# A gated mix of windowed attention and a ReGLU layer, forward and backward: other lengths in the build-time planner, e^z spread by DRAM instead of matmuls

## The chip, the cores and the metric

One core of a Trainium2 chip runs the whole kernel in one launch. The metric is the device time of that launch in microseconds (us). A core has five engines that run side by side, each through its own instruction stream in a fixed order: TensorE (PE, matmuls into eight PSUM banks of 128 x 512 float32), VectorE (DVE), ScalarE (ACT), GpSimd (POOL), and SyncE (SP), which here does nothing but issue transfers. ScalarE and GpSimd issue some transfers too. Transfers run on 16 DMA engines. Engines wait for one another, and for transfers, on semaphores.

## The reference

Sequence S = 2048, width D = 512, 32 heads of 16, a causal window of 256, F = 1376, everything bfloat16.

```python
def attn(x, wqkv, wo):                       # 32 heads, Dh = 16
    q, k, v = split_heads(x @ wqkv)
    scores = (q @ k.T) * Dh ** -0.5          # masked to 0 <= i - j < 256
    return merge_heads(softmax(scores) @ v) @ wo

def ffn(x, W_gate, W_up, W_down):
    gate, up = x @ W_gate, x @ W_up
    return (gate * (gate > 0) * up) @ W_down

z = (x * gate_w).sum(-1, keepdims=True)
g = sigmoid(z)
out = g * attn(x, wqkv, wo) + (1 - g) * ffn(x, W_gate, W_up, W_down)
```

The kernel returns `out` (out_0) and, for a given grad_out, the gradients by x (out_1), wqkv (out_2), wo (out_3), W_gate and W_up (out_4, out_5), W_down (out_6) and gate_w (out_7).

## The kernel before

**The order is planned when the kernel is built.** The Python code doesn't issue instructions one after the other. It lists operations (`op`, `dma`) with what they read and write, a rank (lower goes first), and a length in ns for each engine that could do them, and the method `run` of class `Flow` (L274) plays them in a small event model: an engine that is free takes the ready operation with the lowest rank, an operation counts as done after its length and a `LATENCY` of its engine, and a transfer counts as done when a common DMA clock has moved its bytes (at 240 bytes per ns) and 2300 ns have passed. The order in which the model starts the operations becomes the fixed order of each engine's stream on the chip. So a length in the code changes no instruction, only where it stands, and on which engine where two were given (`either`: ScalarE or VectorE). TensorE's operations have a mode: "row" (scores, one operation is a `slot`), "col" (sweeps) and "den" (dense); a change of mode costs `SWITCH` in the model. The rank of a dense operation gets a small random addition from the list `SEEDS`, one seed for every 200 operations. Where the model has nothing else for TensorE, it puts in a filler matmul (L1569) into a free bank.

**Buffers** are rings in one SBUF tile, `arena`, and the PSUM tile `banks`; an operation that opens a buffer waits in the model until an old one is done. In the profile nearly everything is therefore called `arena` or `banks`, and lines and tile shapes tell operations apart.

**Start (about 0 to 40 us).** The 2048 rows are four blocks `sb` of 512. For each block the kernel loads x (`x_r`) and grad_out (`db_r`), turns x with TensorE into `x_T` (`rows_to_T`), computes z by 16 narrow matmuls (`zf` in `gates`), and on ScalarE e^z, ln(1 + e^z) and 1 - g (`ez_all`, `g_all`, `omg_all`, one number per row, rows on partitions, L840). VectorE multiplies grad_out by 1 - g in place (`sf`, L848), and TensorE turns it into `db_T`. `proj` (L799 to L809) projects 128 columns (8 heads) of K, V and Q out of `x_T` and dO out of `db_T` (by wo), and stores them to DRAM in a layout by heads: `KV_d` and `QD_d`. Since db holds (1 - g) grad_out and the attention's share is g grad_out, the projected dO is multiplied by e^z = g / (1 - g) on the way out of PSUM (L799, VectorE). There rows lie along the columns, so e^z is needed on every partition: `ez_bc`, 128 x 2048. To get it, `gates` lets TensorE multiply `gw_rep` (gate_w repeated in 128 columns) with `x_T`, four matmuls of 512 columns for a block, and ScalarE takes the exponential of the bank (L860):

```python
accumulate(pz, [mm(lambda: pz[:], lambda c=c: gw_rep[:, c, :], lambda c=c: x_T[:, c, sl]) for c in range(DC)],
           [(x_T, sb), gw_rep], 0.8 if sb else 1.6)
op({ACTE: t_act(W)}, lambda e: nc.scalar.activation(ez_bc[:, sl], pz[:], ACT.Exp), r=[pz], w=[(ez_bc, sb)], rank=1)
```

**Attention (about 40 to 709 us).** 16 stages n: four groups of 8 heads, in halves of four heads with four blocks of rows each. `load_stage` loads a stage's K and V (`KV_d`, L975), Q and dO (`QD_d`, L978) and a turned copy by a DMA transpose (L980), from which GpSimd or VectorE copies V beside a column of ones (L987). Work comes in slots (L1049): one slot holds the eight score matmuls of a unit that begins (Q K) and of one that ends (dO V), two heads each, in two units that lie in other rows of the array where possible. After a slot ScalarE takes the exponentials (L1090), GpSimd masks the edge blocks (L1066), VectorE multiplies by the dO V scores (L1096). Sweeps (L1112) are the products of these probabilities with V, Q, K and dO. Between them the model sets dense work: the projections of the other head groups, the gated layer (`front`, L673, L897, L902; `back`), whose activations go through `ffn_d`, and the early products of the last stage (`accumulate_pairs`, L1402).

**End (about 709 to 806 us).** Dense products only: the heads' results come back from `HD_d` by transposes on ScalarE's queue, L1402 forms o and dx for each tile t of 128 rows, partial sums come from `b_d` and `dx_p`; `final` and `whole` finish a tile and store it (L1517 and L1564 are the last stores; GpSimd's additions are L1509 and L1515). The gradient of gate_w is a sum over all 2048 rows: for 13 of the 16 tiles VectorE adds them up in `gx` over the columns' rows (the long sum), which is split into a bfloat16 part and its remainder (`gx2`, the subtraction is L1474 on GpSimd here), and `direct` (L1481) adds both halves and the last three tiles by five matmuls of one bank, copied out (L651, 1 x 512) and stored at the very end.

**Queues.** SP issues nearly all transfers, in the planned order; its issue of a transfer that waits for data holds up all that stand behind it.

Of the kernel before, what the change touches and what calls it, by code (L numbers as in the profile page):

```python
# [10 lines left out]
ALU = mybir.AluOpType  # L11
# [23 lines left out]
def place(segs, dist):  # L35
# [15 lines left out]
LATENCY = {PE: 230, DVE: 130, ACTE: 150, POOL: 100, SP: 2300}  # L51
SWITCH = 98
BACKLOG = 1500
# [3 lines left out]
    51316, 1683, 24937, 57401, 42949, 47415, 22897, 43060, 3505, 15123, 3852, 2860, 11922, 41846, 5348, 49132,  # L57
    25696, 10850, 43592, 31894, 31367, 38632, 11354, 8520, 40074, 25554, 54658,
# [157 lines left out]
class Flow:  # L216
# [57 lines left out]
    def run(self):  # L274
# [3 lines left out]
        now, dma_free, mode, heavy, done = 0.0, 0.0, "", False, 0  # L278
# [42 lines left out]
        while done < len(self.ops):  # L321
            progress = True
            while progress:
                progress = False
                for e in (PE, ACTE, DVE, POOL, SP):
# [3 lines left out]
                    if dma_free > now + BACKLOG:  # L329
                        cands = [o for o in cands if o.rank < 3 or not o.nbytes]  # L330
# [36 lines left out]
                    if o.nbytes:  # L367
                        dma_free = max(dma_free, now + took) + o.nbytes / 240
# [31 lines left out]
def kernel(  # L400
# [42 lines left out]
    MASKV = {DVE: 470, ACTE: 600}  # L443
    DTT = 640
    HQ, OUTS, DIRECT = (SP, ACTE), 2, 3
    COLX, ROWX = 20, 4
# [4 lines left out]
    PAD = 0  # L451
    FRONT, EARLY, BACK, DW, DWO, LAG = 4, 4.6, 4.3, 4.4, 4.5, 3
# [16 lines left out]
    dx_p = [Buf(None, dram.tile([P, D], F32, name=f"dx_p{t}")) for t in range(NT)]  # L469

# [246 lines left out]
    def load_rows(dst, src_d, sb):  # L717
        dma(lambda: nc.sync.dma_start(dst[:, 4 * sb:4 * sb + 4, :],
                                      src_d[sb * W:(sb + 1) * W, :].rearrange("(t p) d -> p t d", p=P)),
            w=[(dst, sb)], nbytes=512 * KB, rank=3)  # L720
# [40 lines left out]
    for sb in range(1, NSB):  # L761
        load_rows(x_r, x_d, sb)
        load_rows(db_r, go_d, sb)
# [48 lines left out]
    def proj_weights(c, deps=()):  # L812
        w3, woT = wsets.pop(("p", c)) if c else wsets["pw", c]
        wi = buf("wi")
        op({POOL: 1200}, lambda e: nc.gpsimd.tensor_copy(wi[:].rearrange("p c (h w d) -> p c w h d", w=2, d=Dh)[:, :, 0],
                                                         w3[:, :, 1, :].rearrange("p c (h d) -> p c h d", d=Dh)),
           r=[(w3, 1)], w=[(wi, 0)], rank=3, deps=deps)
        op({POOL: 1200}, lambda e: nc.gpsimd.tensor_copy(wi[:].rearrange("p c (h w d) -> p c w h d", w=2, d=Dh)[:, :, 1],
# [6 lines left out]
    def gates(sb):  # L825
# [11 lines left out]
        op({PE: 16 * 17}, zf, r=[(x_T, sb), gw_out], w=[zps], rank=0.5 if sb else 1.6, mode="den")  # L837
# [12 lines left out]
        op({DVE: 4 * 200}, sf, r=[gate_b, (db_r, sb)], w=[(db_r, sb)], rank=0)  # L850
# [13 lines left out]
    for sb in range(NSB):  # L864
        later[sb] = rows_to_T(x_T, x_r, sb, 0.2)
# [6 lines left out]
        later["db", sb] = rows_to_T(db_T, db_r, sb, 0.4)  # L872
        proj(0, 3, sb, 1)
    load_ffn(0, [later[0]])
    proj_weights(0, [later["db",3]])

    def front(fc):
        fs = fsz(fc)
        wg, wu, wdT = wsets.pop(("f", fc))
        for tg in range(NSB):  # L880
# [16 lines left out]
            op({DVE: t_stt(W)}, lambda e, q=q, ups=ups: nc.vector.scalar_tensor_tensor(  # L897
# [3 lines left out]
            for k, (a, b) in enumerate((("rg", "upm"), ("dhs", "upm"), ("dhs", "rg"))):  # L901
                op({POOL: t_pool(W, 2), DVE: DTT}, lambda e, q=q, k=k, a=a, b=b: EN[e].tensor_tensor(  # L902
# [68 lines left out]
    def load_stage(n):  # L971
# [15 lines left out]
        op({POOL: 330, DVE: 200}, lambda e: EN[e].tensor_copy(v_of(k1r), v_of(kvr)), r=[kvr, k1r], w=[k1r], rank=1.2)  # L987
# [17 lines left out]
    def units(kind, n):  # L1005
# [9 lines left out]
        for k in range(2 * len(packs)):  # L1015
            u = Unit()
            u.segs, u.runs, width = packs[k // 2]
            u.kind, u.n, u.p, u.r, u.width = kind, n, k // 2, k % 2, width * P
            u.last = k == 2 * len(packs) - 1
            u.Pt = buf("Pt" + kind)  # L1020
            u.S = [buf("S") for _ in range(2)]
            u.dP = u.Pd = None
            us.append(u)
        return us

    def users(kind, n):
        return sets[kind, n] + (sets["A", n + 1][:2] if kind == "N" and joined(n + 1) else [])
# [5 lines left out]
    def score_mms(u, second):  # L1033
# [3 lines left out]
        for i in (2 * u.r, 2 * u.r + 1):  # L1037
            rs = slice(32 * i, 32 * i + (32 if second else Dh))
            lst = []
            for a, b0, cnt, col, kind, n in u.segs:  # L1040
# [6 lines left out]
                def one(lt=lt, ls=ls, rt=rt, rsl=rsl, i=i, rs=rs, cs=slice(col * P, (col + cnt) * P)):  # L1047
                    bank = u.dP[i % 2][:, cs] if second else u.S[i % 2][:, cs]
# [13 lines left out]

    def mask(u):
        for kind, b, cnt, sgn in u.runs:
# [6 lines left out]
    def slot(nxt, cur):  # L1071

        if cur:
            cur.Pd, cur.dP = buf("Pd"), [buf("dP") for _ in range(2)]
        lists, ins, outs = [], [], []
        for u, second in ((cur, True), (nxt, False)):
            if u:
# [9 lines left out]
        if nxt:  # L1087
            w = nxt.width
            for h in range(2):
                op({ACTE: t_act(w)}, lambda e, h=h: nc.scalar.activation(nxt.Pt[:, h, :w], nxt.S[h][:, :w], ACT.Exp),  # L1090
                   r=[nxt.S[h]], w=[(nxt.Pt, h)], rank=0)
            op({POOL: sum(t_pool(2 * cnt * P) for _, _, cnt, _ in nxt.runs)}, lambda e: mask(nxt), r=[nxt.Pt], w=[nxt.Pt], rank=0)
        if cur:
            wc = cur.width
            for h in range(2):
# [502 lines left out]
```

## Time and profile before

| | us |
|---|---|
| three runs, median (lowest to highest) | 805.25 (804.71 to 806.75) |
| the profiled execution, its own time | 807.78 |
| its span, from the first to the last instruction | 806.1 |
| TensorE's share of its full clock in it | 0.999 |
| DMA, bytes moved (mean rate) | 152.18 MB (189 GB/s) |
| scores L1049, TensorE busy (2944 matmuls) | 156.4 |
| sweeps L1112, TensorE busy (2944 matmuls) | 94.6 |
| dense L673, TensorE busy (2000 matmuls) | 393.6 |
| dense pairs L1402, TensorE busy (784 matmuls) | 186.2 |
| score products L1096 on VectorE (740) | 458.2 |
| exponentials L1090 on ScalarE (740) | 395.3 |
| masks L1066 on GpSimd (752) | 354.9 |

The busy times are sums over an engine's instructions; matmuls are pipelined and their ends are modelled, so the sums say how long TensorE had something in it, and the distances between the starts of successive matmuls say how fast it went. The profiled execution is 2.5 us longer than the median of the others; sums made on its trace are therefore compared with its own time, and moved to the median by that difference.

In the lines that follow, `PE`, `DVE`, `ACT`, `POOL` are engines, `SPq` is the issue of a transfer on SP; a line of the timeline gives the start in us, the length in us, engine, line of the code, operation, what is written and read. The lines by stretch give for each the length, the busy time (and count) of PE, weight loads, DVE, ACT and POOL, the granted clock, the share of the DMA engines and their GB/s. The lines of TensorE's waits give the total in us, the count and the longest.

### The profile page before, as it was taken

The page shows a single profiled execution, that of the slowest core. Times are in us where ns is not written, and L with a number is a line of the kernel's source. Part 1 is how long each engine was busy: PE and PEld are TensorE (multiplying, and loading weights), DVE is VectorE, ACT ScalarE, POOL GpSimd, SP SyncE. Part 2 cuts the span into 40 slices and gives each one's busy share as a digit, 9 for nine tenths or more (in the row PEclk, how much of TensorE's full clock was granted, in tenths as well). Part 3 has the DMA queues.
Part 4 walks back from the last instruction along what each step waited for, and adds up shares of the span by engine and source line. Part 5 has one row for each costly group of instructions (what it writes and reads, how often), then busy time and mean ns, then how long its engine had stood idle before and what let it go on. Part 6 is the DMA issues. An engine that isn't in the chain of part 4 may idle for free.

```text
span 806.1 us, 24249 instructions
## 1 busy us (share of the span) xinstructions
PE 791.7 (98%) x8946; PEld 370.9 (46%) x8946; DVE 697.5 (87%) x1249; ACT 600.7 (75%) x1200; POOL 547.5 (68%) x957
## 2 busy tenths in 40 slices
PE   8999999999999999999999999999999999999997
PEld 5543444454354454454545545443434443344443
DVE  3589999999999999999999988999999999927654
ACT  5787798788888788888887888888988888413232
POOL 2388878766898888989997765657666666202246
PEclk9999999999999999999999999999999999999999
DMA  9889558576789887989898798768746766688886
GB/s 241 195 161 243 144 149 183 135 158 129 172 184 217 185 155 190 228 202 198 204 237 190 214 205 173 159 164 207 211 124 155 201 194 143 192 247 211 219 230 202
DMA packets 313009, 152.18 MB, mean 189 GB/s; under 512 B 203161, under 2 KB 303194, under 8 KB 312250
## 3 DMA queue, kind: packets, MB, share of 16 engines
q1 hardware_dynamic: 293938, 136.47, 72.8%
q10 hardware_dynamic: 18456, 12.72, 5.7%
q0 software_dynamic: 496, 1.44, 0.7%
q8 instruction: 70, 1.15, 0.6%
q14 instruction: 49, 0.40, 0.2%
HBM read 55.02 MB, written 55.74 MB: 137 GB/s over the span
## 4 chain that ended last, share of the span: by engine, by line
PE 59%; DMA 5%; POOL 4%; DVE 3%; issue 2%; ACT 2%; SPq 0%; POOLq 0%; DVEq 0%; ACTq 0%
PE banks L673 24%; PE banks L1402 16%; PE banks L1049 11%; PE banks L1112 7%; DMA arena<-b_d 2%; DVE arena L1096 1%; POOL arena L1066 1%; DMA arena<-dx_p 1%; POOL arena L902 1%; ACT arena L1090 1%; POOL arena L1515 1%; DMA arena<-HD_d 1%; PE banks L1147 1%; POOL arena L1509 1%; DMA out_dram<-arena 1%
## 5 line engine op out<-in xcount | busy, mean ns | idle before, releaser
L1096 DVE TENSOR_TENSOR arena<-arena,banks 128x512 bf16<-128x512 bf16 (+1 forms) x740 | 458.2, 665 | 24.4 <-PE banks L1049 21.5
L1066 POOL TENSOR_SCALAR_AFFINE_SELECT arena<-arena 128x256 bf16<-128x256 bf16 (+1 forms) x752 | 354.9, 497 | 151.1 <-ACT arena L1090 132.5
L1090 ACT ACTIVATE arena<-banks 128x512 bf16<-128x512 f32 (+1 forms) x740 | 395.3, 588 | 76.8 <-PE banks L1049 59.4
L673 PE MATMUL banks<-arena 128*128 128x512 bf16 (+4 forms) x2000 | 393.6, 336 | 1.1 <-ACT arena L1090 0.9
L673 PEld LDWEIGHTS <-arena 128*128 128x128 bf16 (+1 forms) x2000 | 175.0, 98 | 154.3 <-issue 55.1
L1402 PE MATMUL banks<-arena 128*128 128x512 bf16 (+1 forms) x784 | 186.2, 380 | 0.0
L1049 PE MATMUL banks<-arena 32*128 32x128 bf16 (+5 forms) x2944 | 156.4, 270 | 4.2 <-DMA arena<-QD_d 1.4
L1049 PEld LDWEIGHTS <-arena 32*128 32x128 bf16 (+1 forms) x2944 | 48.8, 92 | 140.6 <-issue 136.9
L1402 PEld LDWEIGHTS <-arena 128*128 128x128 bf16 (+1 forms) x784 | 69.4, 97 | 89.4 <-issue 17.1
L902 POOL TENSOR_TENSOR arena<-arena 128x512 bf16<-128x512 bf16 (+1 forms) x90 | 104.4, 1164 | 3.8 <-ACT arena L651 1.7
L651 ACT CAST arena<-banks 128x512 bf16<-128x512 f32 (+4 forms) x162 | 77.2, 489 | 31.9 <-PE banks L673 16.2
L1112 PE MATMUL banks<-arena 128*32 128x128 bf16 (+5 forms) x2944 | 94.6, 271 | 1.8 <-POOL arena L987 1.7
L1112 PEld LDWEIGHTS <-arena 128*32 128x32 bf16 (+1 forms) x2944 | 60.5, 94 | 34.6 <-issue 15.9
L1509 POOL TENSOR_TENSOR arena<-arena 128x512 bf16<-128x512 f32 x12 | 16.1, 1341 | 52.1 <-DMA arena<-b_d 26.2
L1143 POOL TENSOR_TENSOR arena<-arena 128x512 bf16<-128x512 f32 x32 | 37.3, 1166 | 11.6 <-issue 8.3
L1508 ACT ACTIVATE arena<-banks,g_all 128x512 f32<-128x512 f32 x12 | 8.2, 688 | 32.1 <-DMA arena<-dx_p 9.8
L902 DVE TENSOR_TENSOR arena<-arena 128x512 bf16<-128x512 bf16 (+1 forms) x42 | 31.3, 749 | 0.4 <-ACT arena L651 0.2
L897 DVE SCALAR_TENSOR_TENSOR arena<-arena,banks 128x512 bf16<-128x512 bf16 (+1 forms) x44 | 29.8, 678 | 1.2 <-PE banks L673 0.8
L653 DVE CAST arena<-banks 128x512 bf16<-128x512 f32 (+1 forms) x38 | 24.4, 644 | 4.1 <-PE banks L673 3.2
L1512 ACT COPY arena<-banks 128x512 f32<-128x512 f32 x12 | 6.9, 587 | 25.0 <-POOL arena L1515 17.0
L1149 DVE SCALAR_TENSOR_TENSOR arena<-arena,vec,banks 128x512 bf16<-128x512 bf16 x32 | 23.6, 737 | 1.4 <-PE banks L1147 1.3
L1141 DVE SCALAR_TENSOR_TENSOR arena<-banks,vec,arena 128x512 bf16<-128x512 f32 x32 | 23.8, 744 | 1.0 <-ACT arena L1140 0.7
(94 smaller groups left out, 403.1 us busy)
## 6 DMA issues: line engine op xcount, KB each, us to landing
ffn_d<-arena SPq DMA_DIRECT2D x40, 384.0 KB
arena<-ffn_d SPq DMA_DIRECT2D x88, 128.0 KB
out_dram<-arena SPq DMA_DIRECT2D x66, 128.0 KB
arena<-HD_d ACTq DMA_DIRECT2D x28, 256.0 KB
KV_d<-arena SPq DMA_DIRECT2D x32, 128.0 KB
QD_d<-arena SPq DMA_DIRECT2D x32, 128.0 KB
arena<-KV_d SPq DMA_DIRECT2D x32, 128.0 KB
arena<-QD_d SPq DMA_DIRECT2D x32, 128.0 KB
```

The lines of the kernel that those rows point to most:

```text
L651: nc.scalar.copy(out, in_)
L653: EN[e].tensor_copy(out, in_)
L673: return lambda start, stop: nc.tensor.matmul(out_fn(), lhsT=lhs_fn(), rhs=rhs_fn(), start=start, stop=stop)
L897: op({DVE: t_stt(W)}, lambda e, q=q, ups=ups: nc.vector.scalar_tensor_tensor(out=q["upm"][:fs, :], in0=q["rg"][:fs, :], scalar=0.0, in1=up ...
L902: op({POOL: t_pool(W, 2), DVE: DTT}, lambda e, q=q, k=k, a=a, b=b: EN[e].tensor_tensor(out=q["act"][:fs, k, :], in0=q[a][:fs, :], in1=q[b] ...
L1049: nc.tensor.matmul(bank, lhsT=lt[rs, ls], rhs=rt[rs, rsl], start=True, stop=True)
L1066: nc.gpsimd.affine_select(out=v.rearrange("p h (b k) -> p h b k", b=cnt), in_=v.rearrange("p h (b k) -> p h b k", b=cnt), compare_op=ALU.i ...
L1090: op({ACTE: t_act(w)}, lambda e, h=h: nc.scalar.activation(nxt.Pt[:, h, :w], nxt.S[h][:, :w], ACT.Exp), r=[nxt.S[h]], w=[(nxt.Pt, h)], rank=0)
L1096: op({DVE: t_dve(wc)}, lambda e, h=h: nc.vector.tensor_tensor(out=cur.Pd[:, h, :wc], in0=cur.Pt[:, h, :wc], in1=cur.dP[h][:, :wc], op=ALU. ...
L1112: nc.tensor.matmul(acc[32 * i:32 * i + wt.shape[1], q0:q0 + cnt * P], lhsT=wt, rhs=m[:, i % 2, col * P:(col + cnt) * P], start=(k == 0), s ...
L1143: op({POOL: t_pool(W, 2), DVE: t_dve(W)}, lambda e: EN[e].tensor_tensor(out=U[:], in0=ri[:], in1=qd[:], op=ALU.mult), r=[ri, qd], w=[U], r ...
L1402: nc.tensor.matmul(bank[:], lhsT=l_(), rhs=r_(), start=(lo + k == 0), stop=(lo + k == n - 1))
```

## The change

1. **The model's numbers.** Latencies, the cost of a switch, and the lengths of a dozen operations are other numbers; transfers issued by GpSimd get a DMA clock of their own, and one that lies beside such a transfer is slower in the model.
2. **e^z for dO** (`EZD = 1`). For each block, SP stores the four columns of `ez_all` to a DRAM buffer `ez_d` of 512 float32, and loads it back to all 128 partitions of `ez_bc`. The four matmuls and the exponential of 128 x 512 of each block are not issued any more (the early `return`); `gw_rep` is still made.
3. **The gate's long sum**: its two matmuls (`direct` on `gx2`) are listed after all tiles, and so come last of the five in the accumulation.
4. **The copies of the projection weights** (`proj_weights`) and the load of the second head group wait for another operation: the turning of grad_out's block 2 instead of block 3 (and of x's).
5. **New seeds**, and so another random addition to every dense operation's rank.
6. **Knobs**: `ROWQ`, `END2`, `START2`, `WIDE`, `TD`, `TDB`, `F0`, `F1`, and slots, units and sweeps rewritten so that a unit may hold both sides of the array. With the values given (`WIDE = 0`, `END2 = 0`, `START2 = 0`, `TD = TDB = 4`, `ROWQ = 9`, `F0 = 0`, `F1 = 1`) they issue what was issued before.

```diff
-LATENCY = {PE: 230, DVE: 130, ACTE: 150, POOL: 100, SP: 2300}
-SWITCH = 98
-BACKLOG = 1500
+LATENCY = {PE: 230, DVE: 135, ACTE: 165, POOL: 100, SP: 2300}
+SWITCH = 97
+BACKLOG, RATE, BY_POOL, BESIDE = 1500, 240, 200, 100
...
 SEEDS = (
-    51316, 1683, 24937, 57401, 42949, 47415, 22897, 43060, 3505, 15123, 3852, 2860, 11922, 41846, 5348, 49132,
+    17664, 1835, 46651, 26643, 54718, 39605, 56992, 30299, 25672, 29398, 19980, 44718, 38679, 30873, 39266, 39201,
...
-                    if dma_free > now + BACKLOG:
+                    if dma_free > now + BACKLOG and e != POOL:
                         cands = [o for o in cands if o.rank < 3 or not o.nbytes]
...
-                    if o.nbytes:
-                        dma_free = max(dma_free, now + took) + o.nbytes / 240
+                    if o.nbytes and e == POOL:
+                        pool_free = max(pool_free, now + took) + o.nbytes / BY_POOL
+                        post(pool_free + LATENCY[SP], "done", o)
+                    elif o.nbytes:
+                        begin = max(dma_free, now + took)
+                        lap = min(max(0, pool_free - begin), o.nbytes / BESIDE)
+                        dma_free = begin + lap + (o.nbytes - lap * BESIDE) / RATE
                         post(dma_free + LATENCY[SP], "done", o)
...
-    MASKV = {DVE: 470, ACTE: 600}
+    MASKV = {DVE: 490, ACTE: 710}
-    COLX, ROWX = 20, 4
+    COLX, ROWX = 3.5, 2.4
...
+    ez_d = [Buf(None, dram.tile([W], F32, name=f"ez_d{sb}")) for sb in range(NSB)]
...
-        op({POOL: 1200}, lambda e: nc.gpsimd.tensor_copy(wi[:].rearrange("p c (h w d) -> p c w h d", w=2, d=Dh)[:, :, 0],
+        op({POOL: 660}, lambda e: nc.gpsimd.tensor_copy(wi[:].rearrange("p c (h w d) -> p c w h d", w=2, d=Dh)[:, :, 0],
...
-        op({PE: 16 * 17}, zf, r=[(x_T, sb), gw_out], w=[zps], rank=0.5 if sb else 1.6, mode="den")
+        op({PE: 16 * 25}, zf, r=[(x_T, sb), gw_out], w=[zps], rank=0.5 if sb else 1.6, mode="den")
...
-        op({DVE: 4 * 200}, sf, r=[gate_b, (db_r, sb)], w=[(db_r, sb)], rank=0)
+        op({DVE: 1060}, sf, r=[gate_b, (db_r, sb)], w=[(db_r, sb)], rank=0)
...
+        sl = slice(sb * W, (sb + 1) * W)
+        if EZD:
+            dma(lambda: nc.sync.dma_start(ez_d[sb][:].rearrange("(t p) -> p t", p=P), ez_all[:, cs_]), deps=[a], w=[ez_d[sb]],
+                nbytes=16 * KB, rank=1)
+            dma(lambda: nc.sync.dma_start(ez_bc[:, sl], ez_d[sb][:].partition_broadcast(P)), r=[ez_d[sb]], w=[(ez_bc, sb)],
+                nbytes=256 * KB, row=2048, rank=1.2)
+            return
         pz = buf("acc")
-        sl = slice(sb * W, (sb + 1) * W)
         accumulate(pz, [mm(lambda: pz[:], lambda c=c: gw_rep[:, c, :], lambda c=c: x_T[:, c, sl]) for c in range(DC)],
...
-    proj_weights(0, [later["db",3]])
+    proj_weights(0, [later["db", 2]])
...
-                op({POOL: t_pool(W, 2), DVE: DTT}, lambda e, q=q, k=k, a=a, b=b: EN[e].tensor_tensor(
+                op({POOL: t_pool(W, 2), DVE: 700}, lambda e, q=q, k=k, a=a, b=b: EN[e].tensor_tensor(
...
-        cols = sum(2 * u.width for u in (cur, nxt) if u) * (2 if nxt and cur and nxt.r == cur.r else 1)
-        wsets["row"] = op({PE: cols / 9.6 + ROWX * count}, lambda e: weave(lists), r=ins, w=outs, order=[prev] if prev else [],
+        wsets["row"] = op({PE: max(cols) / 2.4 + ROWX * count}, lambda e: weave(lists), r=ins, w=outs, order=[prev] if prev else [],
...
-        load_proj(c, [later[3]] if c == 1 else ())
+        load_proj(c, [later["db", 2]] if c == 1 else ())
...
-            for k in range(2):
-                direct(lambda: ones_c[:], lambda k=k: gx2[:, k], [(gx2, k)])
...
+    for k in range(2):
+        direct(lambda: ones_c[:], lambda k=k: gx2[:, k], [(gx2, k)])
     dgs = buf("dgs", [1, D])
```

More of the change, by code (lines that the diff above doesn't have):

```diff
@@ L451 @@
     PAD = 0
+    ROWQ = 9
+    END2 = 0
+    START2 = 0
+    WIDE = 0
+    EZD = 1
+    TD = 4
+    TDB = 4
+    F0 = 0
+    F1 = 1
     FRONT, EARLY, BACK, DW, DWO, LAG = 4, 4.6, 4.3, 4.4, 4.5, 3
@@ L1061, in weave, with part @@
             k += 1
+    def part(u, t_, b):
+        return t_[:, b % 2, b // 2 * u.width:(b // 2 + 1) * u.width]
     def mask(u):
-        for kind, b, cnt, sgn in u.runs:
+        for k, (kind, b, cnt, sgn) in [(k, run) for k in range(len(u.rs)) for run in u.runs]:
+            b += k * u.width // P
             v = u.Pt[:, :, b * P:(b + cnt) * P]
@@ L1093, in slot @@
-        if cur:
-            wc = cur.width
-            for h in range(2):
-                op({DVE: t_dve(wc)}, lambda e, h=h: nc.vector.tensor_tensor(
-                    out=cur.Pd[:, h, :wc], in0=cur.Pt[:, h, :wc], in1=cur.dP[h][:, :wc], op=ALU.mult),
-                    r=[cur.Pt, cur.dP[h]], w=[cur.Pd], rank=0)
+        for u in nxts:
+            for b, bank_ in enumerate(u.S):
+                op({ACTE: t_act(u.width)}, lambda e, u=u, b=b, bank_=bank_: nc.scalar.activation(
+                    part(u, u.Pt, b), bank_[:, :u.width], ACT.Exp), r=[bank_], w=[(u.Pt, b)], rank=0)
+            op({POOL: sum(t_pool(2 * cnt * P) for _, _, cnt, _ in u.runs) * len(u.rs)}, lambda e, u=u: mask(u), r=[u.Pt], w=[u.Pt], rank=0)
@@ L1257 @@
                 tasks_A2(cur.n)
-            elif cur.kind == "A" and cur.j == 1 and joined(cur.n):
+            elif cur.end:
                 tasks_N(cur.n - 1)
```

157 lines of the change are left out of this document (96 added, 61 removed).

## The prediction, made before the changed kernel was run

> **What bounds the kernel now.** I read the busy times first, then the same by stage, the chain of waits, TensorE's own waits, and last the timelines of the start and of the end.
>
> ```profile
> span 806.1 us, 24249 instructions
> PE 791.7 (98%) x8946; PEld 370.9 (46%) x8946; DVE 697.5 (87%) x1249; ACT 600.7 (75%) x1200; POOL 547.5 (68%) x957
> ```
> ```profile
> 0.00:40.00 40.00, 35.72 (x343) 22.11 (x343) 17.74 (x48) 25.10 (x51) 13.38 (x36) 1.00 0.88 218
> 40.00:709.00 669.00, 663.21 (x8168) 305.71 (x8161) 630.16 (x1100) 551.33 (x1097) 499.52 (x896) 1.00 0.80 183
> 709.00:806.00 97.00, 92.79 (x448) 43.04 (x444) 49.59 (x101) 24.23 (x52) 34.57 (x26) 0.99 0.81 220
> ```
> ```profile
> 709.05 37.47 PE banks L1402 x173
> ```
>
> TensorE is busy in all three stages (start, attention, last dense products) at full clock. The piece of the chain gives the price of a 512-column matmul in a stream: 37.47 / 173 = 0.217 us. Since a matmul's end is modelled, I also walked the starts of all 8946 matmuls in the timeline, in which each shape has a regular step (512 columns 0.216, 384 columns 0.163, 256 columns 0.109, eight score matmuls of one slot 0.329, a change from dense work to scores 0.095). The regular steps add up to 778.0 us from the first start to the last, and the starts lie 799.8 us apart: 21.8 us are gaps. Some 6 us of these lie in the first 40 us (slow steps up to 9 us, a wait for x of 1.5, the wait shown below), eight gaps over 0.35 us between 40 and 720 us make 7.9 us, a dozen slots whose two units share the same rows of the array 2.6 us, and from 720 us on there are none. So a TensorE microsecond that is taken away is worth a microsecond, unless a gap takes its place; only gaps can turn the result.
>
> ```profile
> PE banks L1112 <- POOL arena L987: 1.7, 1, 1.7
> PE banks L1049 <- DMA arena<-QD_d: 1.4, 1, 1.4
> PE banks L1049 <- DVE arena L1141: 1.3, 1, 1.3
> PE banks L673 <- ACT arena L1090: 0.9, 1, 0.9
> ```
> The reader should see that these are single events, and that each names a late transfer or an engine behind one: L987 copies V out of a transfer from KV_d.
>
> **The change, part by part.** *Removed: sixteen matmuls.* In `gates`, 4 blocks x 4 matmuls of 512 columns that spread z = x.gate_w over 128 partitions, with 4 exponentials (L860). 16 x 0.217 = 3.5 us of TensorE, all of it on the path. ScalarE's 4 x 0.60 us are hidden: in the first 40 us it is busy 25.1.
>
> *Added: eight transfers on SP.* For each block a store of 128 x 4 numbers to `ez_d` and a load of 2 KB to each of 128 partitions. On SP a store like it (QD_d, below) takes about 0.6 us to issue and a plain load 0.34 to 0.53: 4 x 1.0 = 4 us of SP over the first 40 us. The loads bring 1 MB; at the 218 GB/s of this stage that is 4.8 us of the DMA engines, which are at 0.88 there. What waits for it is this:
>
> ```profile
> 13.12 0.60 ACT L860 ACTIVATE arena<-banks 128x512 f32<-128x512 f32 x1
> 22.00 1.29 SPq L809 DMA_DIRECT2D QD_d<-arena  x2
> 23.33 0.53 SPq L718 DMA_DIRECT2D arena<-in_grad_out_dram  x1
> 28.71 0.34 SPq L978 DMA_DIRECT2D arena<-QD_d  x1
> 31.47 1.14 DVE L848 TENSOR_SCALAR arena<-arena,omg_all 128x512 bf16<-128x512 bf16 x4 [1.07 <-DMA arena<-in_grad_out_dram]
> 33.57 0.41 PE L1049 MATMUL banks<-arena 16*128 16x384 bf16 x8 [1.41 <-DMA arena<-QD_d]
> ```
>
> Now e^z of block 0 is there at 13.72. VectorE multiplies it into the projected dO (L799, 21.1), the product goes to QD_d (22.0 to 23.3), and the load of 28.71 brings it back for the first scores at 33.57. In the new order of SP, e^z's store for block 0 stands behind three stores of K, V, Q; its load behind two 512 KB loads, a K/V load, a DMA transpose and the store for block 1; the dO part's store behind the store for block 2; and the load of QD_d eight transfers later, past the dO load of block 3 and a transpose. Behind the waiting multiply on VectorE stand the scaling of dO block 2 and a copy that frees a bank of TensorE's.
>
> The first scores are matmul 283 now, after 25.9 us of regular steps, and TensorE is ready for them at 32.1. In the new order they are matmul 277, after 24.6 us: ready at 30.8. The way there: e^z's store at about 12.8 (its exponential follows the same matmuls as L840 now); its load behind the transpose that now ends issuing at 18.7 and the store for block 1, so about 19.4; 4 to 5 us to land, as the QD_d load of 28.71 needs 4.9; the multiply, 0.7, to 24.2; its store 0.6 and 3 to 6 us to land (now 22.7 to 28.7 at most); the load 3 to 5 us. That puts the first scores between 30.8 (no wait, if the loads are short) and 36. I take 33.3: a wait of 2.5 where it is 1.5 now, **+1.0**. From below: the wait goes altogether, -1.5. From above: both trips take 8.1 us each, as the dO load of 23.33 does that L848 waits for at 31.47; that is the slower rival.
>
> The Trainium skill (DMA: Bandwidth & Descriptors, Rules for kernel authors) says that a transfer whose last dimension is strided becomes one descriptor per element, and tells authors to rearrange it. That speaks against the store to `ez_d`: 512 pieces of 4 bytes. No row of this trace shows such a store. As an estimate, at the 32 ns that a packet takes on queue 1 on average (72.8% of 16 engines over 806.1 us for 293938 packets) it holds each engine for 1.0 us; by this rule the sum below would be -2.8 and the time 802.4.
>
> *Moved: the whole order.* The planner's lengths and seeds change no instruction, only where it stands. I counted both built orders. TensorE keeps 2944 score and 2944 sweep matmuls; its runs of one kind go from 821 to 818, fewer sweeps are split (87 to 78 runs), more changes go from dense work to scores (330 to 338). In regular steps the new order is 3.9 us shorter up to the last matmul that is needed, so **-0.4** beside the sixteen matmuls. Whether the gaps between 40 and 720 us grow is the unknown. I counted for every transfer how much TensorE work lies between the last matmul that it needs and the first that needs it. Past the start, room under 7 us is left 4 times now and 5 times then, under 9 us 23 and 22 times. The K/V transpose with 6.3 to 7.4 us of room stays the tightest kind. So I take **0** for these gaps, with -4 (half of them gone) and +4 (half as many again) as ends. VectorE, at 630 of 669 us in this stage, keeps its 740 score products; its count changes by ten instructions.
>
> *Moved: the gate's long sum.* The five matmuls of the gate's gradient end TensorE's work in both orders, so this puts no work on the path. But the subtraction ahead of them leaves GpSimd for VectorE:
>
> ```profile
> 785.07 1.16 POOL L1474 TENSOR_TENSOR arena<-arena 128x512 bf16<-128x512 f32 x1 [3.47 <-PE banks L1402]
> 800.78 1.26 POOL L1515 TENSOR_TENSOR arena<-arena 128x512 bf16<-128x512 f32 x1
> 800.85 0.57 ACT L651 CAST arena<-banks 1x512 bf16<-1x512 f32 x1 [0.59 <-PE banks L1481]
> 802.07 0.33 SPq L1517 DMA_DIRECT2D out_dram<-arena  x1
> 803.26 0.43 SPq L1564 DMA_DIRECT2D out_dram<-arena  x1
> ```
> GpSimd's last addition ends at 802.04; SP waits for it before it can issue the two last stores. The gradient is copied by 801.42; without that wait its store could go 1.8 us earlier. GpSimd loses 1.16 us and a wait in that chain; I take half, **-0.9** (ends 0 and -1.8). The reader should also see what is late next: the last transpose of HD_d now issues 44 us before the end (761.64) and is used at 775.3. In the new order it can't issue before a store that needs work 13 us of TensorE ahead of its use, where it now has 14. That still covers it.
>
> **The sum**: -3.5 - 0.4 - 0.9 + 1.0 = **-3.8 us**, against the span of 806.1 (1.7 us lie around it, 807.78 in that execution): 802.3. The three unprofiled runs have a median of 805.25, so **801.4**.
>
> **The rivals.** *(B) The better lengths also shorten the gaps.* The eight gaps are places where the planner expected an engine earlier: 7.9 us, half of them gone is -4, and **797.4**. For: one of them is a multiplication on VectorE planned at 640 ns and now at 700. Against: the others hang on transfers, and the rate of SP's transfers stays at 240 in the model.
>
> *(C) The start takes the saving back.* The first scores come at 36.2, 5.4 us after TensorE is ready: +3.9, nothing left, **805.2**. For: DMA at 0.88 and SP in order. Against: e^z of the first block has 8 us until the dO product needs it.
>
> *(D) Slower: e^z's two trips are late.* If both take 8.1 us, the load lands at 19.4 + 8.1 = 27.5 (the store is back by 20.9, and 1.5 of that is lost as well: 29.0), the product is stored by 30.3, lands by 36 and is loaded by 40.9: a wait of 10.1 instead of 1.5, so -3.5 - 0.4 - 0.9 + 8.6 = +3.8: **809.1**. It turns slower where the first scores start after 36.2, and by 0.3% after 38.6. For: the 8.1 us of the dO load in this very stretch. Against: that load moves 512 KB, e^z's 256 KB. The Trainium skill (TensorE: Matmul & The Clock Gate, The HAM clock gate) adds that an idle window of about 3.4 us halves the clock; by it this case would be worse by up to 1.7 us. The trace can't show it: its waits are 1.7 us at most and the clock stays at 1.00.
>
> **Chances.** Forecast 0.52 (799 to 803.5), B 0.17, C 0.17, D 0.14. What this kernel's measurement can tell is 0.3%, 2.4 us. Faster by more (below 802.8): 0.45 of the forecast, B, 0.02 of C: 0.64. Slower by more (above 807.7): 0.13 of D. The rest is 0.23. The range takes in B's middle and C with the lower part of D: 796 to 807.
>
> **What would show it.** Sixteen dense matmuls of 512 columns fewer in the group of L673; no exponentials of 512 columns in `gates`; first scores near 33 us; the wait for QD_d 1 to 4 us; gaps between 40 and 720 us of 8 us together; the last store issued less than a microsecond after the gradient's copy. The prediction is wrong if the first scores start after 36 us, if single waits of TensorE in the attention stage add up to more than 12 us or less than 4, or if TensorE stands still in the last 90 us.

## The result, and the profile after

The changed kernel takes **844.07 us** (median of 4 runs, 837.37 to 849.42), the kernel before beside it 805.50 us (4 runs, 804.71 to 806.75): a ratio of 1.047 with a 95% interval of 1.039 to 1.055. The forecast was 801.4 us. Rival D, the slower one, was given 809.1 us, 3.8 us more than before; what came is ten times that, 38.6 us more. The profiled execution took 846.16 us with a span of 844.5.

Busy times, then the same by stage (length, busy time and count of PE, weight loads, DVE, ACT and POOL, granted clock, share of the DMA engines, GB/s), then TensorE's waits, all of the changed kernel:

```profile
span 844.5 us, 24068 instructions
PE 788.8 (93%) x8822; PEld 372.6 (44%) x8929; DVE 697.1 (83%) x1256; ACT 596.0 (71%) x1187; POOL 548.3 (65%) x959
```
```profile
0.00:40.00 40.00, 24.03 (x210) 16.35 (x214) 10.29 (x33) 13.65 (x26) 9.26 (x25) 0.87 0.96 149
40.00:100.00 60.00, 39.27 (x273) 16.87 (x274) 26.25 (x47) 27.52 (x53) 24.95 (x45) 0.80 0.97 144
100.00:747.00 647.00, 632.17 (x7871) 296.00 (x7967) 611.67 (x1069) 531.64 (x1061) 479.46 (x864) 1.00 0.76 181
747.00:845.00 98.00, 93.38 (x475) 43.41 (x475) 48.94 (x109) 23.14 (x48) 34.60 (x25) 1.00 0.90 222
```
```profile
PE banks L1089 <- DMA arena<-QD_d: 14.1, 1, 14.1
PE banks L793 <- DMA arena<-in_A_x_dram: 7.6, 3, 5.8
PE banks L793 <- DVE arena L868: 6.3, 1, 6.3
PE banks L689 <- DMA arena<-in_B_W_down_dram: 5.1, 1, 5.1
```
```profile
62.55 0.62 PE L1089 MATMUL banks<-arena 16*128 16x384 bf16 x8 [14.06 <-DMA arena<-QD_d]
```

TensorE is busy 24.0 of the first 40 us (before: 35.7) and 39.3 of the next 60 (before: 60.0 of that stretch). Yet the DMA engines are at 0.96 and 0.97 while they move 149 and 144 GB/s: before they moved 218 GB/s at 0.88. So packets take up their time, yet little moves. The share adds up the times of all packets, so it can pass 1 where these overlap. The first scores (the last line) wait 14.1 us for QD_d; they start at 62.55 us instead of 33.57. And the clock, which stood at 1.00 before, is granted at 0.87 and 0.80.

The walk along the starts of TensorE's matmuls, as in the prediction, puts the difference into four parts (us; a matmul whose record is missing is counted by its regular step; the tail is from the last matmul's start to the end of the span):

| | before | after | difference | predicted |
|---|---|---|---|---|
| regular steps | 777.8 | 773.7 | -4.1 | -3.9 |
| gaps, 0 to 100 us | 7.2 | 47.7 | +40.5 | +1.0 |
| gaps, later | 14.8 | 18.9 | +4.1 | 0 (-4 to +4) |
| tail | 4.7 | 2.6 | -2.1 | -0.9 |

The loss is in the start. These are the transfers of e^z on SP in the changed kernel (start of the issue in us, its length), transfers of QD_d beside them, and the three multiplies on VectorE that wait for e^z (the last bracket is the idle time ahead):

```profile
13.04 0.42 SPq L878 DMA_DIRECT2D ez_d<-ez_all  x1
...
22.55 0.57 SPq L878 DMA_DIRECT2D ez_d<-ez_all  x1
24.44 0.34 SPq L880 DMA_DIRECT2D arena<-ez_d  x1
24.88 0.62 SPq L829 DMA_DIRECT2D QD_d<-arena  x1
...
38.31 0.34 SPq L880 DMA_DIRECT2D arena<-ez_d  x1
38.74 0.57 SPq L878 DMA_DIRECT2D ez_d<-ez_all  x1
39.36 1.62 SPq L829 DMA_DIRECT2D QD_d<-arena  x2
...
59.19 0.34 SPq L1013 DMA_DIRECT2D arena<-QD_d  x1
```
```profile
38.49 0.69 DVE L819 TENSOR_TENSOR arena<-banks,arena 128x512 bf16<-128x512 f32 x1 [8.92 <-DMA arena<-ez_d]
...
51.80 0.69 DVE L819 TENSOR_TENSOR arena<-banks,arena 128x512 bf16<-128x512 f32 x1 [7.99 <-DMA arena<-ez_d]
...
63.18 0.69 DVE L819 TENSOR_TENSOR arena<-banks,arena 128x512 bf16<-128x512 f32 x1 [0.21 <-DMA arena<-ez_d]
```

The first store of 2 KB is issued at 13.04, and its load can go at 24.44: the store landed at 24.43, 11.4 us after its issue. The next three took 15.7, 19.9 and 12.5 us. Meanwhile other transfers are slow as well. The first load of e^z lands at 38.40, 14.0 us after its issue. Block 0's dO can then be multiplied (38.49); its store, the first of the two issued from 39.36, lands at 59.12, 19.8 us later. The load for the first scores goes at 59.19 and lands at 62.50. A store to QD_d that doesn't need e^z, issued at 24.88, lands at 40.41. In the trace's records of single packets, the 1,160 packets of 1 KB that start between 10 and 14 us take 53 ns each on average; after a burst of 4-byte packets at 29 us, the 20 that start between 31 and 34 us take 2,577 ns each.

### The profile page after: what moved, and what is told of

The parts are those of the page before. It is cut to its first block, busy times and chain, and to the rows that moved or that the text cites. A ratio compares the mean times of both kernels' runs of the same rounds, so it can differ in the third digit from the quotient of the medians.

```text
span 844.5 us, 24068 instructions
## 1 busy us (share of the span) xinstructions
PE 788.8 (93%) x8822; PEld 372.6 (44%) x8929; DVE 697.1 (83%) x1256; ACT 596.0 (71%) x1187; POOL 548.3 (65%) x959
## 5 line engine op out<-in xcount | busy, mean ns | idle before, releaser
L1140 DVE TENSOR_TENSOR arena<-arena,banks 128x512 bf16<-128x512 bf16 (+1 forms) x740 | 456.6, 665 | 19.4 <-PE banks L1089 13.9
L689 PE MATMUL banks<-arena 128*128 128x512 bf16 (+4 forms) x1913 | 384.4, 336 | 11.5 <-DMA arena<-in_B_W_down_dram 5.1
L1467 PE MATMUL banks<-arena 128*128 128x512 bf16 (+1 forms) x748 | 181.6, 380 | 4.9 <-issue 2.1
L1089 PE MATMUL banks<-arena 32*128 32x128 bf16 (+5 forms) x2944 | 158.2, 271 | 17.9 <-DMA arena<-QD_d 14.1
L667 ACT CAST arena<-banks 128x512 bf16<-128x512 f32 (+4 forms) x161 | 78.5, 498 | 30.5 <-PE banks L689 21.5
L1022 POOL COPY arena<-arena 128x256 bf16<-128x256 bf16 x25 | 9.9, 395 | 53.2 <-DMA arena<-KV_d 52.3
L1571 ACT ACTIVATE arena<-banks,g_all 128x512 f32<-128x512 f32 x12 | 8.2, 684 | 35.1 <-PE banks L1467 14.3
L667 ACT COPY arena<-banks 128x512 f32<-128x512 f32 (+3 forms) x20 | 14.2, 719 | 24.6 <-PE banks L793 18.5
L1023 ACT ACTIVATE arena<-arena,vec 128x512 bf16<-128x512 bf16 x21 | 17.2, 818 | 16.7 <-DMA arena<-KV_d 16.7
L669 DVE CAST arena<-banks 128x512 bf16<-128x512 f32 (+3 forms) x39 | 22.7, 592 | 7.0 <-PE banks L1156 3.0
```

Source lines behind the costliest of these rows:

```text
L667: nc.scalar.copy(out, in_)
L669: EN[e].tensor_copy(out, in_)
L689: return lambda start, stop: nc.tensor.matmul(out_fn(), lhsT=lhs_fn(), rhs=rhs_fn(), start=start, stop=stop)
L1089: nc.tensor.matmul(bank, lhsT=lt[rs, ls], rhs=rt[rs, rsl], start=True, stop=True)
L1140: op({DVE: t_dve(u.width)}, lambda e, u=u, b=b, bank_=bank_: nc.vector.tensor_tensor(out=part(u, u.Pd, b), in0=part(u, u.Pt, b), in1=bank_ ...
L1467: nc.tensor.matmul(bank[:], lhsT=l_(), rhs=r_(), start=(lo + k == 0), stop=(lo + k == n - 1))
```

## The experiments

Each ran beside the kernel before on one chip. In the ratios the interval is 95%.

### Is it e^z's way through DRAM, and what of it?

```diff
-    EZD = 1
+    EZD = 0
```


> The changed kernel with EZD = 0: the sixteen matmuls and the exponentials of 128 x 512 are back, the stores to ez_d and the loads from it are gone, and lengths, seeds and the gate's long sum stay as changed. Theory S (small pieces: after each burst of 512 packets of 4 bytes to ez_d the trace of the changed kernel shows 10 us in which packets of 1 KB take 300 to 3000 ns instead of 46): the loss of 38 us goes with the stores, 803 to 808 us. Rival T (the trips: two transfers in a row through SP's queue are late whatever their pieces): the same here. Rival O (the new order outside e^z's path has made the start slower): 830 us or more.

Measured: 820.16 us (816.93 to 827.14), ratio 1.020 (1.014 to 1.027). None of the three: the start is healed (gaps of 9.9 us in the first 100, first scores at 30.82), but 15 us are still lost. This order has 25 filler matmuls, since the planner planned anew with seeds sought for another kernel; the second group below takes that up.

```diff
-            dma(lambda: nc.sync.dma_start(ez_d[sb][:].rearrange("(t p) -> p t", p=P), ez_all[:, cs_]), ...
+            dma(lambda: nc.sync.dma_start(ez_d[sb][:].rearrange("(p t) -> p t", t=4), ez_all[:, cs_]), ...
...
-                nc.vector.tensor_tensor(out=cs[:], in0=pp[:], in1=ez_bc[:, sl], op=ALU.mult)
+                nc.vector.tensor_tensor(..., in1=ez_bc[:, sl].rearrange("q (p t) -> q t p", t=4), op=ALU.mult)
```


> The changed kernel, but e^z goes to ez_d as it lies in SBUF, four numbers of a partition side by side: 128 pieces of 16 bytes instead of 512 of 4; the load to 128 partitions is as before, and the multiply on VectorE reads it with a step of four numbers. Same instructions, same order. Theory S, if the cost goes by the number of pieces: a quarter of the slow stretch, 2.5 us for each store, 803 to 815 us. Rival T: both trips are still there, 835 us or more. Rival B (the load of the same 2 KB to 128 partitions is what slows the DMA engines): 835 us or more.

Measured: 817.41 us (812.01 to 819.95), ratio 1.014 (1.009 to 1.019). That is 2 us above the end of theory S's range. The stores land in 4.4 to 5.7 us. With the same instructions in the same order, other pieces of the same 2 KB are worth 26.7 us. The load to 128 partitions is still there, so it isn't the cause of these (rival B), nor are the two trips as such (rival T). Some 12 us are still lost.

```diff
+            def turn(e):
+                for k in range(2):
+                    nc.tensor.matmul(pt[:4, :P], lhsT=ez_2[:, sb, k], rhs=ident[:], start=k == 0, stop=k == 1)
...
+            wsets["ezd", sb] = dma(lambda: nc.sync.dma_start(ez_d[sb][:].rearrange("(t p) -> t p", p=P), ez_r[:4, sb % 2, :]), ...
```


> The changed kernel, but e^z is turned by TensorE first (split in two bfloat16 parts, two matmuls of 128 columns) and copied to four partitions, so that the store to ez_d has four pieces of 512 bytes; load and multiply as in the changed kernel. The order is planned anew. Theory S: no slow stretch, 800 to 808 us. Rivals T and B: store and load are both there, and one step more ahead of them, 830 us or more.

Measured: 816.90 us (816.02 to 823.44), ratio 1.016 (1.011 to 1.020). That is 9 us above theory S's range, though the slow stretch is gone: the stores land in 2.8 to 5.2 us. The gaps of the first 100 us are 12.2 us, where the kernel before has 7.2 and the run with the matmuls back 9.9. So the trips seem to cost 2 to 5 us even so; since the order was planned anew, no run shows it alone.

```diff
+        def send():
+            nc.sync.dma_start(dst[c][sb][:].rearrange("(h w d) s -> w h d s", w=2, d=Dh)[k], cs[:])
+            if c == 0 and which == 3:
+                nc.sync.dma_start(ez_d[sb][:].rearrange("(t p) -> p t", p=P), ez_all[:, 4 * sb:4 * sb + 4])
```


> The kernel before, in its own order, with only the four stores to ez_d added (512 pieces of 4 bytes each), each issued by SP right behind the store of the block's dO part; nothing reads them. Theory S: each store slows all transfers for some 10 us between 23 and 45 us, and TensorE waits for K, V, Q: 820 to 845 us. Rivals T and B: nothing waits for these stores and nothing is loaded, 805 to 808 us.

Measured: 834.67 us (831.90 to 838.94), ratio 1.036 (1.031 to 1.041). Four stores of 2 KB that nobody reads cost the old order 29.6 us. The stretch from 23 to 46 us, in the kernel before and here, and TensorE's longest wait here:

```profile
23.00:46.00 23.00, 21.59 (x209) 10.44 (x208) 13.36 (x29) 18.26 (x40) 10.31 (x23) 1.00 0.83 181
```
```profile
23.00:46.00 23.00, 12.46 (x120) 7.79 (x121) 6.64 (x17) 9.20 (x19) 3.79 (x9) 0.81 1.42 118
```
```profile
PE banks L1055 <- DMA arena<-QD_d: 14.9, 2, 10.3
```
Transfers move 118 GB/s instead of 181, and TensorE is busy for 12.5 us instead of 21.6.

### What about the small pieces is slow?

```diff
-                nc.sync.dma_start(ez_d[sb][:].rearrange("(t p) -> p t", p=P), ez_all[:, 4 * sb:4 * sb + 4])
+                nc.sync.dma_start(ez_d[sb][:, 0].rearrange("(t p) -> p t", p=P), ez_all[:, 4 * sb:4 * sb + 4])
```
(`ez_d[sb]` is now 512 x 128 float32.)

> As the run with the four dead stores in the kernel before (834.7 us against 805.1), but each of the 512 numbers of a store goes to a place of its own, 512 bytes from the next. Theory P (each piece costs some 20 ns, whatever its size and place: 10 us for 512): 828 to 842 us. Theory Z (it is the small size, 4 bytes, that is slow, wherever it goes): the same, 828 to 842. Theory L (pieces that different DMA engines write side by side hinder each other): 804 to 809 us.

Measured: 805.15 us (804.00 to 808.85), ratio 1.001 (0.998 to 1.003). The whole cost is gone, with as many pieces of the same size, so neither their number (P) nor their size (Z) alone is what costs. The same stretch:

```profile
23.00:46.00 23.00, 23.00 (x218) 10.89 (x216) 14.65 (x31) 19.44 (x43) 11.29 (x24) 1.00 0.80 177
```

```diff
+                nc.sync.dma_start(ez_d[sb][:P].rearrange("(t p) -> p t", p=P), ez_all[:, 4 * sb:4 * sb + 1])
```


> As the run with the four dead stores, but only one column is stored for each block: 128 pieces of 4 bytes side by side instead of 512. All of theories P, Z and L: a quarter of the slow stretch, some 2.5 us for each store, which the 30 us lost shrink to 3 to 8: 806 to 813 us. A fixed cost for each store of this form: 825 us or more.

Measured: 827.74 us (823.37 and 832.10), ratio 1.026 (1.013 to 1.040). With two executions the time itself is rough, but a quarter of the pieces costs nearly as much as all. P, Z and L as I had priced them all miss. What was named as a fixed cost for each store of this form fits; since the store apart costs nothing, that can't be a cost of every store, only of one whose pieces lie side by side.

```profile
23.00:46.00 23.00, 12.79 (x122) 7.61 (x122) 6.64 (x16) 8.54 (x20) 4.07 (x9) 0.78 1.42 121
```

```diff
+                nc.sync.dma_start(ez_d[sb][:].rearrange("t p k -> p t k"), ident[:, :32].rearrange("p (t k) -> p t k", t=4))
```


> As the run with the four dead stores, with as many pieces, 512 for each store, but 16 bytes each instead of 4 (of constants that lie in SBUF anyway, stored side by side in the same interleaved manner). Theory P: 828 to 842 us. Theory Z: 804 to 810 us. Theory L: in between, since fewer pieces share the same stretch of DRAM: 808 to 828 us.

Measured: 808.79 us (806.48 to 812.91), ratio 1.005 (1.003 to 1.008). This lies in the ranges of both Z and L, and the store apart has ruled Z out.

The time from the issue of each of the four stores to its landing (us, from the semaphores' records) puts the four runs together:

| store | pieces | side by side | landing, four stores | time |
|---|---|---|---|---|
| as in the change | 512 of 4 bytes | yes | 11.3, 15.0, 14.0, 13.5 | 834.7 |
| one column | 128 of 4 bytes | yes | 11.3, 15.3, 13.8, 12.4 | 827.7 |
| wider | 512 of 16 bytes | yes | 6.4, 6.6, 4.1, 4.7 | 808.8 |
| apart | 512 of 4 bytes | 512 bytes apart | 4.7, 4.9, 2.8, 3.4 | 805.2 |

The best reading is that it counts how many pieces fall on the same short stretch of DRAM, not how many there are. A column of 128 numbers fills 512 bytes with 128 pieces, and four such columns do it four times over, side by side, in the same time. With 16 bytes a stretch of 512 bytes takes 32 pieces, and lands nearly as fast as those apart. So of the three theories L is the one left, with the correction that different stretches seem to be served beside each other. What is shown is that lying side by side makes the cost (4 bytes, 512 pieces, only the place differs: 834.7 against 805.2 us). The rest is argued: with 16 bytes the size changed along with the number in a stretch, and how long the stretch is, or what serves it one piece at a time, was not measured. The Trainium skill (DMA: Bandwidth & Descriptors, Specifications) says that below 512 bytes a DMA engine reads, modifies and writes; by that rule alone pieces of 4 bytes would be slow wherever they go, and the store apart shows that they aren't.

### What the new lengths and the search are worth

```diff
-    EZD = 1
+    EZD = 0
...
-    17664, 1835, 46651, 26643, 54718, 39605, 56992, 30299, 25672, 29398, 19980, 44718, 38679, 30873, 39266, 39201,
+    17664, 26335, 40265, 3116, 5990, 21967,
...
```


> The run with the matmuls back (820.2 us; the planner's own model ended it at 808.2 us with 25 filler matmuls, since its seeds had been sought for another kernel), with seeds sought for it: the model now ends at 794.1 us with 5 fillers. The model ended the kernel before at 802.6 (span 806.1, 3.5 us more) and the changed one at 791.3 (span 844.5; 813.6, 22 us more, in the run with pieces of 16 bytes). Theory M (the lengths set to the trace leave the model no slack, so every late event stays in the order: the chip ends 8 to 22 us after the model): 804 to 818 us. Rival F (the lengths are right and only the search was missing: 3 to 5 us after the model, and 1.7 around the span): 798 to 801 us.

Measured: 807.35 us (804.84 to 812.97), ratio 1.004 (1.002 to 1.006). So the new lengths with an order sought for them, without e^z's trips, are no faster than the kernel before. Theory M's range holds it, and rival F's doesn't. Against 820.16 us, other seeds alone are worth 12.8 us here.

```diff
-    EZD = 1
+    EZD = 0
...
-    COLX, ROWX = 3.5, 2.4
+    COLX, ROWX = 20, 4
```
(and seeds sought for it)

> The run with the matmuls back (820.2 us, model 808.2, span 816.4), but with the two lengths COLX and ROWX as before (20 and 4 instead of 3.5 and 2.4 ns for each sweep and score matmul), and seeds sought until the model ended at the same time, 807.9 us. Theory M (these two lengths held the slack): the span 2 to 5 us after the model, 811 to 815 us. Rival F, or slack in other places: 817 to 823 us, as with the short lengths.

Measured: 808.27 us (805.47 to 810.67), ratio 1.003 (1.001 to 1.005); the profiled span was 804.1 us. That is even less than expected, against 820.16 with the short lengths and the same end in the model.

| | model's end | chip's span | chip less model | gaps after 100 us |
|---|---|---|---|---|
| kernel before (20, 4) | 802.6 | 806.1 | +3.5 | 14.8 |
| long lengths back (20, 4) | 807.9 | 804.1 | -3.8 | 14.6 |
| matmuls back (3.5, 2.4) | 808.2 | 816.4 | +8.2 | 21.5 |
| search without trip (3.5, 2.4) | 794.1 | 809.8 | +15.7 | 19.8 |
| pieces of 16 (3.5, 2.4) | 791.3 | 813.6 | +22.3 | 19.7 |
| diagonal on VectorE, below (20, 4) | 802.9 | 801.6 | -1.3 | 14.4 |

The model's ends come from the planner itself. All profiles of orders with the short lengths have 18.9 to 21.5 us of gaps behind the first 100 us, those with the long ones 14.3 to 15.9. The likely reason is that with the two lengths of before the chip catches up with the plan after a late event, while with the shorter ones the plan runs as fast as the chip can and a late event stays; one profile for each order doesn't prove it. In four of these profiles (matmuls back, pieces of 16, one column, and one matmul of ones below) a stretch of 3.4 us at half clock behind 100 us adds up to 1.7 us, which doesn't close the difference. (With 25 fillers against 7, the 820.16 us hold more than this; the gaps are the cleaner measure.) The slack is no gain in time by itself: the searched order with short lengths took 807.35 us, the one with long lengths 808.27, and the model had ended 13.8 us earlier for the first.

### The tail, and versions that might beat both

```diff
-            op({POOL: t_pool(W, 2), DVE: DTT}, lambda e: EN[e].tensor_tensor(
+            op({DVE: DTT}, lambda e: EN[e].tensor_tensor(
                 out=gx2[:, 1], in0=gx[:], in1=gx2[:, 0], op=ALU.subtract), ...
```


> The kernel before, all in its place, but the subtraction of the gate's long sum is done by VectorE instead of GpSimd; no other instruction moves. The step of the prediction: GpSimd's last addition ends 1.2 us or more earlier, SP's last two stores follow, 0.9 to 1.8 us less: 803.3 to 804.4 us. Rival: the end hangs on something else in these last microseconds (TensorE, the gradient's copy), 805.0 to 805.5 us.

Measured: 804.52 us (803.37 to 806.78), ratio 0.9994 (0.998 to 1.001): not told apart from no change. And the run with the stores apart, which still has the subtraction on GpSimd, ends like this (GpSimd's last addition, ScalarE's copy of the gradient, the last store):

```profile
797.72 1.26 POOL L1521 TENSOR_TENSOR arena<-arena 128x512 bf16<-128x512 f32 x1
...
800.43 0.57 ACT L653 CAST arena<-banks 1x512 bf16<-1x512 f32 x1 [0.58 <-PE banks L1487]
801.04 0.26 SPq L1570 DMA_DIRECT2D out_dram<-arena  x1
```
GpSimd is done at 798.98, 2 us before the copy ends. In the profiled execution of before its last addition ended 0.6 us after the copy. In the profiles of the three other runs that keep this order to the end (dead stores, one column, 16 bytes), GpSimd is done 2.0 to 2.4 us before the copy's end as well. The late GpSimd was that one execution's, not the order's.

```diff
+            if sb:
+                nc.scalar.copy(z_all[:, cs_], zps[:, 0:4])
+                for k in range(4):
+                    nc.scalar.mul(gw_rep[:, k, :], ident[:], z_all[:, 4 * sb + k:4 * sb + k + 1])
...
+                nc.tensor.matmul(pz[:], lhsT=ones_m[:], rhs=gw_rep[:].rearrange("p t k -> p (t k)"), start=True, stop=True)
```


> As the run with the subtraction on VectorE, and for blocks 1 to 3 the four matmuls that spread z are replaced by one: ScalarE multiplies the identity by z (four instructions of 128 x 128 and a small copy), and a matmul of ones with that matrix of 512 columns puts z on all partitions. Nothing goes through DRAM; nine matmuls of 0.217 us fewer, 2.0 us, if no gap takes their place. If TensorE's microseconds at the start are worth a microsecond each: 801.3 to 802.5 us. Rival: the first scores wait for QD_d anyway and take it back, 803.3 to 804.4 us; or ScalarE's 1.2 us more for each block delay what it does next, and it is slower than without: 805 us or more.

Measured: 806.40 us (805.81 to 810.86), ratio 1.002 (1.000 to 1.003), by the second rival:

```profile
PE banks L868 <- ACT ez_all L847: 4.7, 3, 1.6
```
TensorE waits three times for the small instructions on ScalarE, 4.7 us in all, for 2.0 us of matmuls saved. The profiled execution is the slowest of the 13 (810.86 us): in it the clock also fell to half three times for 3.4 us, so its gaps are larger than those of the median.

```diff
+        op({DVE: 680}, lambda e: nc.vector.tensor_tensor(
+            out=dz4[:], in0=ident[:].unsqueeze(1).to_broadcast([P, 4, P]), in1=bc(zps[:, 0:4], P), op=ALU.mult), ...
```


> The kernel before with its own lengths (COLX 20, ROWX 4), the gate's long sum last, and for all four blocks one matmul of ones with a diagonal matrix of z that VectorE makes in one instruction of 128 x 512 (the planner knows of it, unlike in the run where ScalarE made it and TensorE waited 1.7 us for it three times); seeds sought until the model ended at 802.9 us (before: 802.6). Twelve matmuls fewer. Theory M (with these lengths the chip ends 4 us before to 3.5 us after the model, as in the kernel before and the run with the long lengths): a span of 799 to 806.4, 800.5 to 808 us, most likely 804: the planner's time, not the matmuls taken away, decides. Rival: each matmul taken away is worth its 0.217 us on the chip whatever the model says: 802.7 us or less.

Measured: 804.98 us (802.76 to 806.52), ratio 0.999 (0.997 to 1.001): no change that can be told, with twelve matmuls fewer. It lies in theory M's range and not in the rival's. No version tried is measurably faster than the kernel before.

## Why the prediction was wrong

- **Sixteen matmuls removed, and the regular steps: right.** -4.1 us measured against -3.9. The weight loads of dense work fell from 2000 to 1984.
- **e^z's transfers: wrong, and this is the step that failed.** The prediction walked the path to the first scores and gave it +1.0 us; the gaps of the first 100 us grew by 40.5. Its legs: e^z's store at 12.8 with its load at 19.4, so at most 6.6 us for the store; the load 4 to 5 us; the store of the product 0.6 and 3 to 6; the last load 3 to 5; scores at 33.3. Measured: 11.4, 14.0, 19.8 and 3.3 us, scores at 62.55. So the starts of the path were right (the store went at 13.04), and the times to land were wrong, of e^z's store and of the two transfers behind it that run beside other such stores. The prediction had named the store of "512 pieces of 4 bytes each", said that no row shows such a store, and priced it in a sentence apart at 32 ns for a packet, 1.0 us for each engine. Measured: 11.4 to 19.9 us for the four stores, and other transfers slow meanwhile. The four dead stores show that this alone costs 29.6 us in the old order, and the stores apart that it hangs on the pieces lying side by side. The slowest price that the prediction took, for rival D, was the 8.1 us of a dO load; but that was a price for bytes, and this store has hardly any. The rule of the Trainium skill that the prediction cited there (DMA: Bandwidth & Descriptors, Rules for kernel authors: one descriptor for each element of a strided last dimension) pointed at the right store, but not at the cause: the store apart has as many pieces and costs nothing. The price put on the store was too small by a factor of more than ten, and it was left out of the range.
- **Rival D had the place right and the size wrong.** Both trips late, the first scores after 36.2: yes (62.55). It priced the trips alone, 8.6 us. It left out that the store hinders its neighbours, and the clock. Of the clock it said at most 1.7 us. The clock stood at half for four stretches of 6.8, 6.8, 13.7 and 6.8 us; a dense step of 512 columns takes 0.427 us in the first, 0.216 else. In these 34 us TensorE did 10.7 us of regular steps, which took 10.7 us more than at full clock; that is the most the clock can have cost, since some of it ran ahead of a wait for a transfer. The first stretch begins at 23.0, 3.8 us into a wait of 5.9 that begins at 19.25: the Trainium skill (TensorE: Matmul & The Clock Gate, The HAM clock gate), which speaks of a window of 3.4 us, agrees with that. But so long a wait isn't needed: in the profile of one matmul of ones the clock fell to half for 3.4 us at 19.59 and 29.83, each time 1.1 to 1.3 us after a wait of only 1.6 us.
- **Gaps between 40 us and the end: 0 taken, +4.1 after 100 us.** Just past the end of the range given (+4). The prediction had counted the room of transfers, and between 100 and 760 us TensorE's waits indeed name no transfer. The larger gaps go with the short lengths of scores and sweeps in all profiles, so rival B (better lengths shorten the gaps) looks the wrong way round.
- **The gate's long sum: right in sign by the profile (-2.1), but not a gain of the change.** The term was read off a single execution whose end was disturbed; the same order ends 2.2 us after the last matmul's start in four other profiles, 4.7 in that one.

What stays open: how the 12 us that are left with pieces of 16 bytes (817.4 against 805.1) divide between the trips and the order. The walk gives 8.7 us more gaps in the start, 4.9 later, 4.1 fewer regular steps and 2.0 less tail; that is an account of the 7.5 us between two profiled executions, not an experiment for each.

## What to carry to other kernels

Don't write a column of single numbers from many partitions side by side into DRAM: turn it first, so that each piece is a row, store it as it lies (here 16 bytes a partition), or leave the pieces apart (512 bytes here). Price an operation that no row shows by what it can do to its neighbours, not by its bytes; where a warning and a small estimate meet, the range must hold the warning. A plan that ends earlier in the model need not end earlier on the chip: here orders planned with lengths somewhat too long had some 3 to 7 us less of gaps behind the first 100 us, and ended as early as an order whose model ended 13.8 us sooner.

## What was not expected of the hardware

A store of 512 bytes, as 128 numbers of 4 bytes side by side, takes 11 to 15 us to land, about as long as four times as many. Such stores bring the transfers of the core from 181 down to 121 GB/s over 23 us. Placed 512 bytes apart, 512 numbers land in 2.8 to 4.9 us and cost nothing that can be measured (805.15 against 805.35 us).

A wait of TensorE of 1.6 us was twice followed by 3.4 us at half clock (one matmul of ones, 19.59 and 29.83), and once, at 37.38, it wasn't.
